# Moving closing copies, output scaling and half sums in a convolution and two-layer network kernel built on fast matrix products

## The chip, the core and the metric

The kernel runs on one core of one Trainium2 chip. The metric is device time in microseconds (us), from the first to the last instruction of the program; lower is better. A core has a matrix engine (TensorE, PE in the profile; its weight loads are listed apart as PEld), a vector engine (VectorE, DVE), a scalar engine (ScalarE, ACT), a general engine (GpSimd, POOL) and a queue engine (SyncE, SP). Each takes its own instructions strictly in the order in which the program lists them, and they wait for one another by semaphores. Matrix products land in PSUM, here eight banks of 512 float32 for each of 128 partitions; everything else lives in SBUF or in DRAM.

## The reference, cut to what matters

```python
# x: (8, 4224, 192), weight: (8 heads, 7 taps)
w = softmax(weight, axis=-1)
y[b, s, 24*h:24*h+24] = sum over k of w[h, k] * x_pad[b, s + k, 24*h:24*h+24]
# x_pad: six zero rows ahead of x, so each row sees itself and the six before it
mu, var = mean and variance of y over its 192 columns
xn = (y - mu) / sqrt(var + 1e-6) * g_ln
out = y + maximum(xn @ w_ch1, 0) @ w_ch2       # (192 x 768), (768 x 192)
```

The factor 1/sqrt(var) passes through the maximum with zero, so the kernel multiplies un-normalised rows and scales the result of the second product. Mean and `g_ln` are folded into the first weight matrix at the start.

## The kernel before

**Groups.** The rows are cut into 18 groups; a full group is 2048 rows, 16 row slots (`J`) for each of 128 partitions. Groups 0 to 2 are small or partial and do ordinary products. Groups 3 to 17 are "mixed": both products of the network are done by a fast scheme with seven products of half-size blocks in place of eight, at the price of sums and differences of blocks ahead of and behind the products. This document is about those 15 groups; the last of them, group 17, does part of its second product in the ordinary way (`down`) and has a short ending of its own.

**A group's first product** is `up_mixed(g)` (lines 585 to 725). It runs in two passes, each with seven calls of `product` (line 521 underneath), each into one of two sets of four PSUM banks, X and Y, in turn:

- pass `one` is the small set: one third of the hidden width (`PAIR` = 2, so f = 2 alone);
- pass `two` is the rest (f = 0 and 1) and takes twice as long.

The hidden layer of a group is one SBUF tile, `room`, seen as `a[:, h, e, f]` with h, e in {0, 1}. Its quarters are called c11 = a[h0, e0], c12 = a[h0, e1], c21 = a[h1, e0] and c22 = a[h1, e1], each with the part of pass one (f = 2) and of pass two (f = 0, 1). A bank set is emptied in one of two ways. `evict` is an ACT copy from PSUM into a quarter. `close` adds a bank set to a quarter that already holds something. A close with a spare part is done as an ACT copy into that part and a POOL-issued DMA that adds the part to the quarter in SBUF (line 583). A close without one is a DVE addition straight from PSUM (line 622). In pass one all three closes have a part; in pass two the first two do, and the last, of c21 from X, is the DVE one. The last group closes everything on DVE.

Before the change the parts of pass one lie in a tile of the pool `tb` (line 647). That pool has one buffer. It also holds, for the group after next, the result of the convolution's second tap (`second_tap`, line 394), which two DMAs add to `y` (line 397). The parts of pass two lie in tiles of the pools `cs` (also the result of the second product) and `tb`.

**The quarters after that.** c12 gets its maximum with zero when it is evicted; c11 and c22 get it by ACT instructions in place (line 629); for c21 `lower_sum` (line 773, DVE) forms max(c21, 0) - c11.

**A group's second product** is `down_fast(g, ...)` (lines 780 to 849), seven calls of its own `product` (line 797), called P1 to P7 below in the order in which they stand. Each is three chunks of columns, and each chunk goes to one bank: P1, P5, P6 and P7 accumulate in banks 0, 2 and 4, P2, P3 and P4 in banks 1, 3 and 5. After each chunk of all but P4 an ACT copy (line 803) takes the bank out. P1 reads c11, P2 the lower sum a[h1, e0], P3 and P5 c22, P4 and P7 c12, P6 c11. Between P4 and P5 nine DVE `half_sum` instructions (line 764) rewrite c22, c11 and c12 in place; the first three write c22, which P5 reads, the next three c11, for P6, and the last three c12, for P7.

**What is woven between.** The engines other than PE also work ahead on the next groups, and the order is written out by hand:

- ACT: two taps of the convolution of group g + 2 (lines 383 and 394), and the scaling of the output of group g - 1, one instruction for each of 16 row slots (`scale`, line 882). When rows 0 to 7 and 8 to 15 are scaled, `add_to_out` (line 889) has POOL issue a DMA that adds them to DRAM, where `y` lies already.
- DVE: taps 2 to 6 of group g + 1 (line 408, 40 instructions for a full group), its `transpose` (line 419), its statistics (`moments`, line 439), sums of its blocks (lines 578 and 579, with 575 and 576 on POOL), and the end of the second product of group g - 1 (`finish_fast`, lines 855 and 857). The transposes of line 857 write the output tile `ot`; its pool has one buffer, so they wait until both `add_to_out` transfers of the group before have read it.

In `down_fast` this weaving was done by `ending(step)` (scaling and adding of g - 1) and `some_taps(n)`.

Of the kernel before, what the change touches and what calls it, by code (L numbers as in the profile page):

```python
# [16 lines left out]
def kernel(  # L17
# [567 lines left out]
    def up_mixed(g, ahead):  # L585


        W = HJ * C
        last = g + 1 == NG
        assert groups[g][2] == 2 * HJ and PAIR * W == 512 and FC == PAIR + 1  # L590
        hidden_tile(g)
        a = ht[g]
        a11, a12, a21, a22 = quarters_of_y(g)
        s1, s2, s3, s4 = ysums[g]
        done = groups[g - 1][2]

        class Pass:
            def __init__(self, f0, f1, chain, other):
                self.n, self.chain, self.other = f1 - f0, chain, other
                self.b11, self.b12, self.b21, self.b22 = quarters_of_w1(f0, f1)  # L600
                self.t = [v[:, :, P * f0 : P * f1] for v in (w1sums[:, k] for k in range(3))]
                (self.c11, self.c12), (self.c21, self.c22) = [
                    [a[:, h, e, f0:f1].rearrange("p f q j t -> p f q (j t)") for e in range(2)]
                    for h in range(2)
                ]

            def product(self, to, left, right, first=True, end=True):
                rows_of_tiles(to, left, right, first, end, True)

            def seen(self, banks):  # L610
                src = banks[:, :, 0 : self.n * W]
                return src.rearrange("p q (f w) -> p f q w", w=W)

            def evict(self, banks, dst, relu=False):
                src = self.seen(banks)
                nc.scalar.activation(dst, src, AF.Relu) if relu else nc.scalar.copy(dst, src)  # L616

            def close(self, c, banks, part=None):


                if part is None or last:
                    nc.vector.tensor_tensor(c, c, self.seen(banks), op=ALU.add)  # L622
                    return
                self.evict(banks, part)
                whole = "p f q w -> p (f q w)"
                add_by_dma(c.rearrange(whole), part.rearrange(whole))

            def relu(self, c):
                nc.scalar.activation(c, c, AF.Relu)  # L629

        def parts(pool, tag):

            room = pool.tile([P, J * D], F32, tag=tag, name=f"parts_{tag}{g}")
            return room.rearrange("p (f q w) -> p f q w", q=NQ, w=W)

        def act_scales(j1, j2):
            if not last:
                scale(g - 1, j1, j2)

        def taps_of_next(*args, **kw):  # L640
            if not last:
                conv(g + 1, *args, **kw)


        X, Y = take_set(), take_set()
        one, two = Pass(PAIR, FC, X, Y), Pass(0, PAIR, Y, X)
        room1 = parts(bpool, "tb")

        p = one
        p.product(X, a11, p.b11, True, False)  # L650
        p.evict(X, p.c11)
        p.product(Y, a12, p.b21)
        p.close(p.c11, Y, room1[:, 0:1])
        p.product(X, s2, p.t[0], False, False)
        p.evict(X, p.c21)
        p.product(Y, s3, p.t[1], True, False)
        p.evict(Y, p.c22)
        p.product(X, s1, p.b12, False, False)
        p.close(p.c22, X, room1[:, 1:2])
        p.product(Y, a22, p.t[2], False)  # L660
        p.close(p.c21, Y, room1[:, 2:3])
        p.product(X, s4, p.b22, False)
        p.evict(X, p.c12, True)

        next(ahead)

        p = two
        room2 = parts(cpool, "cs")
        room3 = parts(bpool, "tb")
        p.product(Y, a11, p.b11, True, False)  # L670
        p.evict(Y, p.c11)
        act_scales(0, 1)
        p.product(X, a12, p.b21)
        p.close(p.c11, X, room2[:, 0:PAIR])
        act_scales(1, 2)
        if last:

            for j1 in (0, HJ):
                part, factor = ots[g - 1][:, j1 : j1 + HJ], rstd[g - 1][:, j1 : j1 + HJ]
                nc.vector.tensor_tensor(  # L680
                    part, part, factor.unsqueeze(2).to_broadcast([P, HJ, D]), op=ALU.mult
                )
                add_to_out(g - 1, j1, j1 + HJ)
        p.product(Y, s2, p.t[0], False, False)
        p.evict(Y, p.c21)
        act_scales(2, 3)
        p.product(X, s3, p.t[1], True, False)
        p.evict(X, p.c22)
        one.relu(one.c11)
        one.relu(one.c22)  # L690
        p.product(Y, s1, p.b12, False, False)
        taps_of_next(2, 5)
        taps_of_next(5, 6, heads=(0, H // 2))
        p.close(p.c22, Y, room3[:, 0:PAIR])
        p.product(X, a22, p.t[2], False)
        taps_of_next(5, 6, heads=(H // 2, H))
        p.relu(p.c11)
        p.close(p.c21, X)
        p.product(Y, s4, p.b22, False)
        p.evict(Y, p.c12, True)  # L700
        lower_sum(g, (PAIR,))
        lower_sum(g, range(PAIR))
        if last:

            rest = a[:, 1, 0, :, :, fast[g] :]
            for f in range(FC):
                nc.scalar.activation(rest[:, f], rest[:, f], AF.Relu)
        taps_of_next(6, K)

        def ending(step):  # L710


            if step == 0:
                two.relu(two.c22)
            if last:
                return
            cuts = [min(j, done) for j in (3, 6, 10, 13, J)]
            if step < len(cuts) - 1:
                scale(g - 1, cuts[step], cuts[step + 1])
            if step == 1:  # L720
                add_to_out(g - 1, 0, 8)
            if step == 3:
                add_to_out(g - 1, 8, done)

        return ending

    po = {}

# [48 lines left out]
        else:  # L777
            half_sum(g, (1, 0), (1, 0), (0, 0), ALU.subtract, fs)

    def down_fast(g, ending):  # L780
        n = fast[g]
        t = width(g)
        w = n * T
# [5 lines left out]
        parts = [free[:, 0:CH], free[:, CH : 2 * CH]]  # L789
        banks = [take_bank() for c in range(CH) for i in range(2)]  # L790

        def product(bank, left, right, to, first):
            for c in range(CH):
                dst = banks[2 * c + bank]
                for f in range(FC):
                    for q in range(NQ):
                        nc.tensor.matmul(  # L797
                            dst[C * q : C * q + C, 0:w], right[:, f, C * c : C * c + C],
                            left[:, f, q], start=(first and f == 0), stop=(f == FC - 1),
                            skip_group_check=True,  # L800
                        )
                if to is not None:
                    nc.scalar.copy(  # L803
                        to[:, c], dst[:, 0:w].rearrange("p (j t) -> p j t", t=t)
                    )

        b = quarters_of_w2()
        c11, c21 = cs[:, 0:CH, 0], cs[:, 0:CH, 1]
        c12, c22 = cs[:, CH:NC, 0], cs[:, CH:NC, 1]
        todo = [(tap, h) for tap in (first_tap, second_tap) for h in range(H)] if g + 2 < NG else []  # L810

        def some_taps(times):
            for tap, h in todo[:times]:
                tap(g + 2, heads=(h, h + 1))
            del todo[:times]

        product(0, a[:, 0, 0], b[0], c11, True)
        ending(0)
        product(1, a[:, 1, 0], w2sums[:, 2], c22, True)
        ending(1)  # L820
        product(1, a[:, 1, 1], w2sums[:, 3], c21, False)
        some_taps(4)
        product(1, a[:, 0, 1], b[2], None, True)
        some_taps(6)
        if g + 1 < NG:
            transpose(g + 1)
            sums = sums_of_y(g + 1, nc.gpsimd)
            next(sums)
            moments(g + 1)
        half_sum(g, (1, 1), (1, 1), (1, 0), ALU.add)  # L830
        half_sum(g, (0, 0), (1, 1), (0, 0), ALU.add)
        half_sum(g, (0, 1), (0, 1), (1, 1), ALU.subtract)
        for c in range(CH):
# [1 line left out]
                c11[:, c], c11[:, c], banks[2 * c + 1][:, 0:w].rearrange("p (j t) -> p j t", t=t),  # L835
                op=ALU.add,
            )
        product(0, a[:, 1, 1], w2sums[:, 1], parts[0], False)
        some_taps(6)
        ending(2)  # L840
        product(0, a[:, 0, 0], w2sums[:, 0], parts[1], False)
        some_taps(len(todo))
        ending(3)
        product(0, a[:, 0, 1], b[3], c12, False)
        if g + 1 < NG:
            next(sums)
        else:
            finish_fast(g, 0, flat, cs, parts)
# [31 lines left out]
    def scale(g, j1, j2):  # L880
        for j in range(j1, j2):
            nc.scalar.mul(ots[g][:, j, :], ots[g][:, j, :], rstd[g][:, j : j + 1])  # L882
# [72 lines left out]
    for g in range(NG):  # L955
# [1 line left out]
        if g + 2 < NG:  # L957
            load_x(g + 2)
        if mixed:
            ending = up_mixed(g, ahead(g))  # L960
        else:
            up(g)
        if not fast[g]:
# [28 lines left out]
            continue  # L992
        if g + 2 < NG:
            store_y(g + 1)
        results = down_fast(g, ending)
        if last:
            finish_fast(g, 1, *results)
            add_and_store(g, slice(0, fast[g]))
# [37 lines left out]
```

## Time and profile before

| | before |
|---|---|
| time, median of 3 runs | 1087.65 us (1085.58 to 1089.54) |
| span of the profiled run | 1085.9 us |
| PE busy | 977.6 us, 90% |
| DVE busy | 893.3 us, 82% |
| ACT busy | 685.6 us, 63% |
| POOL busy | 230.5 us, 21% |
| DMA queue of POOL (q0), share of 16 engines | 46.7% |
| DMA queue of SP (q1), share of 16 engines | 17.1% |
| mean granted TensorE clock | 0.987 |
| first product of group 3 starts at | 123.18 us |
| first product of group 4 | 182.50 us |
| first product of group 16 | 959.12 us |
| first product of group 17 | 1023.04 us |

The profile gives busy time by engine. A PE that counts as busy may still be running its pipeline empty: in a steady group of 65.05 us (376.73 to 441.78) the busy time is 56.66 us. The last rows of the table are start times of the instruction group `ps<-yt,w 32*128 32x256` that opens a mixed group, from the timeline of PE; the difference of two of them is the time of a whole group, whatever happened in it. A line of the timeline gives start, duration, engine, line, operation, output and input, number of instructions, and in brackets the idle time ahead of it with what the profile takes for its releaser. Each float32 matrix product of the program appears as two instructions.

### The profile page before, as it was taken

The page shows a single profiled execution, that of the slowest core. Times are in us where ns is not written, and L with a number is a line of the kernel's source. Part 1 is how long each engine was busy: PE and PEld are TensorE (multiplying, and loading weights), DVE is VectorE, ACT ScalarE, POOL GpSimd, SP SyncE. Part 2 cuts the span into 40 slices and gives each one's busy share as a digit, 9 for nine tenths or more (in the row PEclk, how much of TensorE's full clock was granted, in tenths as well). Part 3 has the DMA queues.
Part 4 walks back from the last instruction along what each step waited for, and adds up shares of the span by engine and source line. Part 5 has one row for each costly group of instructions (what it writes and reads, how often), then busy time and mean ns, then how long its engine had stood idle before and what let it go on. Part 6 is the DMA issues. An engine that isn't in the chain of part 4 may idle for free. (4 is left out here: it accounts for less than half of the span.)

```text
span 1085.9 us, 38303 instructions
## 1 busy us (share of the span) xinstructions
PE 977.6 (90%) x17274; PEld 740.3 (68%) x17274; DVE 893.3 (82%) x1491; ACT 685.6 (63%) x1083; POOL 230.5 (21%) x383
## 2 busy tenths in 40 slices
PE   7999998999888988898899889898898999889998
PEld 5876575857667575675758567585675858567687
DVE  6999986995959879595996959789595986959777
ACT  5646575776757676676776657577475766657361
POOL 1015204121130211311123110412123121130300
PEclk9999999999999999999999999999899999999999
DMA  8352968578585877758668675866768577574331
GB/s 182 105 205 38 241 139 205 108 206 168 169 171 104 222 137 202 147 144 193 135 194 160 189 153 113 218 129 196 147 174 179 119 208 146 128 141 87 58 61 61
DMA packets 26385, 165.14 MB, mean 152 GB/s; under 512 B 3567, under 2 KB 4463, under 8 KB 18542
## 3 DMA queue, kind: packets, MB, share of 16 engines
q0 software_dynamic: 19120, 99.36, 46.7%
q1 hardware_dynamic: 6798, 63.34, 17.1%
q8 instruction: 135, 2.21, 0.8%
q14 instruction: 28, 0.23, 0.1%
q10 hardware_dynamic: 304, 0.00, 0.0%
HBM read 38.95 MB, written 50.33 MB: 82 GB/s over the span
## 5 line engine op out<-in xcount | busy, mean ns | idle before, releaser
L408 DVE SCALAR_TENSOR_TENSOR y<-xg,taps,y 128x384 f32<-128x384 f32 (+3 forms) x734 | 366.9, 580 | 1.0 <-ACT y L383 0.8
L797 PE MATMUL ps<-room,w2sums 128*32 128x256 f32 (+1 forms) x4320 | 241.0, 375 | 17.5 <-DVE room L764 16.5
L521 PE MATMUL ps<-yt,w 32*128 32x256 f32 (+2 forms) x4104 | 240.5, 381 | 0.0
L521 PEld LDWEIGHTS ps<-yt,w 32*128 32x128 f32 x4104 | 208.5, 188 | 25.8 <-issue 7.0
L797 PEld LDWEIGHTS ps<-room,w2sums 128*32 128x32 f32 x4320 | 146.0, 110 | 108.5 <-DVE room L764 34.0
L797 PE MATMUL ps<-room,w 128*32 128x256 f32 (+1 forms) x3240 | 182.6, 378 | 35.7 <-issue 12.6
L797 PEld LDWEIGHTS ps<-room,w 128*32 128x32 f32 x3240 | 112.9, 110 | 100.5 <-issue 17.9
L857 DVE STREAM_TRANSPOSE ot<-cs 128x512 f32<-128x512 f32 (+1 forms) x90 | 55.9, 672 | 152.5 <-DMA out_dram<-ot 104.1
L616 ACT COPY room<-ps 128x1024 f32<-128x1024 f32 (+1 forms) x90 | 129.6, 1440 | 75.9 <-PE ps L521 75.9
L521 PE MATMUL ps<-ysums,w1sums 32*128 32x256 f32 x2160 | 135.0, 395 | 35.7 <-ACT parts_tb L616 35.7
L764 DVE TENSOR_TENSOR room<-room 128x1024 f32<-128x1024 f32 (+1 forms) x135 | 151.9, 1200 | 6.1 <-ACT cs L803 6.1
L521 PEld LDWEIGHTS ps<-ysums,w1sums 32*128 32x128 f32 x2160 | 112.9, 192 | 52.2 <-ACT parts_tb L616 41.4
L803 ACT COPY cs<-ps 128x256 f32<-128x256 f32 (+1 forms) x180 | 63.8, 366 | 99.9 <-PE ps L797 98.0
L616 ACT COPY parts_tb<-ps 128x1024 f32<-128x1024 f32 (+1 forms) x56 | 68.5, 1223 | 57.4 <-DMA y<-tb 44.8
L583 POOL DMA_DIRECT2D room<-parts_tb x56 | 48.3, 862 | 249.9 <-ACT parts_tb L616 177.2
L882 ACT ACTIVATE ot<-ot,r 128x192 f32<-128x192 f32 x232 | 90.9, 449 | 0.0
L629 ACT ACTIVATE room<-room 128x1024 f32<-128x1024 f32 (+1 forms) x60 | 87.5, 1486 | 1.4 <-DMA room<-parts_tb 1.4
L889 POOL DMA_DIRECT2D out_dram<-ot x40 | 35.0, 1098 | 235.5 <-ACT ot L882 205.7
L383 ACT ACTIVATE y<-xg,taps 128x384 f32<-128x384 f32 (+3 forms) x141 | 70.3, 586 | 8.4 <-DMA out_dram<-y 6.9
L521 PE MATMUL ps<-ysums,w 32*128 32x256 f32 x1080 | 65.8, 382 | 6.5 <-ACT parts_tb L616 6.5
L439 DVE BATCH_NORM_STATS2 st<-y 128x6 f32<-128x192 f32 x264 | 69.7, 342 | 0.0
L803 ACT COPY room<-ps 128x256 f32<-128x256 f32 (+1 forms) x90 | 30.2, 364 | 60.6 <-PE ps L797 57.4
(102 smaller groups left out, 897.4 us busy)
## 6 DMA issues: line engine op xcount, KB each, us to landing
xg<-in_x_dram SPq DMA_DIRECT2D x15, 2112.0 KB, 14.8
out_dram<-ot POOLq DMA_DIRECT2D x29, 768.0 KB, 12.3
y<-tb POOLq DMA_DIRECT2D x28, 768.0 KB, 9.1
room<-parts_tb POOLq DMA_DIRECT2D x42, 512.0 KB, 5.5
out_dram<-y SPq DMA_DIRECT2D x13, 1536.0 KB, 6.1
room<-parts_cs POOLq DMA_DIRECT2D x14, 1024.0 KB, 7.5
room<-parts_tb POOLq DMA_DIRECT2D x14, 1024.0 KB, 7.2
xg<-in_x_dram SPq DMA_DIRECT2D x1, 1536.0 KB, 7.9
```

The lines of the kernel that those rows point to most:

```text
L383: nc.scalar.mul(y[g][:, 0:n, cs], xg[g][:, 0:n, cs], taps[:, h, 0:1])
L408: nc.vector.scalar_tensor_tensor(out=y[g][:, 0:n, cs], in0=t[:, k : k + n, cs], scalar=taps[:, h, k : k + 1], in1=y[g][:, 0:n, cs], op0=AL ...
L439: nc.vector.bn_stats(out=sums[g][:, j, :], in_=y[g][:, j, :])
L521: nc.tensor.matmul(banks[:, q, i * w : i * w + w], right[rows, c, P * i : P * i + P], left[rows, :, c, :], start=(first and c == 0 and i = ...
L583: nc.gpsimd.dma_start(out=dst, in_=src, accum_op=ALU.add)
L616: nc.scalar.activation(dst, src, AF.Relu) if relu else nc.scalar.copy(dst, src)
L629: nc.scalar.activation(c, c, AF.Relu)
L764: nc.vector.tensor_tensor(a[:, *dst, f], a[:, *left, f], a[:, *right, f], op=op)
L797: nc.tensor.matmul(dst[C * q : C * q + C, 0:w], right[:, f, C * c : C * c + C], left[:, f, q], start=(first and f == 0), stop=(f == FC - 1 ...
L803: nc.scalar.copy(to[:, c], dst[:, 0:w].rearrange("p (j t) -> p j t", t=t))
L857: nc.vector.transpose(ot[:, 0:n, C * c : C * c + C], flat[:, c].rearrange("p (j t) -> p j t", t=C))
L882: nc.scalar.mul(ots[g][:, j, :], ots[g][:, j, :], rstd[g][:, j : j + 1])
```

## The change

Six edits belong to it. (1) The three closing copies of pass one go to places in `room` that pass two will only write later: the c12 and c22 of pass two. The tile of the pool `tb` for them is gone. (2) In pass two the scaling of the rows of group g - 1 moves by one place each, four rows instead of three are scaled there, and the two `relu` of pass one that stood ahead of the close of c22 move: that of c11 behind this close, that of c22 to the second product. (3) On DVE four of the convolution's instructions move from ahead of the last close to behind it, and the first `lower_sum` moves from behind this close to ahead of it. (4) In `down_fast` one list, `work`, replaces `ending` and `some_taps`. It holds the rest of the `relu`s, the scaling row by row, and the taps, and it is taken from after each chunk, so that the scaling and both `add_to_out` are behind P1 and P2, where they were spread up to behind P6. The `relu` of c22 becomes two halves. (5) Inside a chunk the part f = 2 of pass one is taken first. (6) `moments` and the block sums of the next group move behind the half sums, from ahead of them.

```diff
-        room1 = parts(bpool, "tb")
...
-        p.close(p.c11, Y, room1[:, 0:1])
+        p.close(p.c11, Y, two.c12[:, 0:1])
...
-        p.close(p.c22, X, room1[:, 1:2])
+        p.close(p.c22, X, two.c12[:, 1:2])
...
-        p.close(p.c21, Y, room1[:, 2:3])
+        p.close(p.c21, Y, two.c22[:, 0:1])
...
         p = two
-        room2 = parts(cpool, "cs")
-        room3 = parts(bpool, "tb")
+        rooms = parts(cpool, "cs"), parts(bpool, "tb")
         p.product(Y, a11, p.b11, True, False)
         p.evict(Y, p.c11)
+        p.product(X, a12, p.b21)
+        p.close(p.c11, X, rooms[0][:, 0:PAIR])
         act_scales(0, 1)
-        p.product(X, a12, p.b21)
-        p.close(p.c11, X, room2[:, 0:PAIR])
-        act_scales(1, 2)
...
         p.evict(Y, p.c21)
-        act_scales(2, 3)
+        act_scales(1, 2)
         p.product(X, s3, p.t[1], True, False)
         p.evict(X, p.c22)
-        one.relu(one.c11)
-        one.relu(one.c22)
+        act_scales(2, 3)
         p.product(Y, s1, p.b12, False, False)
         taps_of_next(2, 5)
         taps_of_next(5, 6, heads=(0, H // 2))
-        p.close(p.c22, Y, room3[:, 0:PAIR])
+        p.close(p.c22, Y, rooms[1][:, 0:PAIR])
+        act_scales(3, 4)
         p.product(X, a22, p.t[2], False)
-        taps_of_next(5, 6, heads=(H // 2, H))
+        one.relu(one.c11)
         p.relu(p.c11)
+        lower_sum(g, (PAIR,))
         p.close(p.c21, X)
         p.product(Y, s4, p.b22, False)
         p.evict(Y, p.c12, True)
-        lower_sum(g, (PAIR,))
         lower_sum(g, range(PAIR))
...
+        taps_of_next(5, 6, heads=(H // 2, H))
         taps_of_next(6, K)
-        def ending(step):
...
+        work = [lambda: one.relu(one.c22)]
+
+        def scale_one(j):
+            scale(g - 1, j, j + 1)
+            if j == 7:
                 add_to_out(g - 1, 0, 8)
-            if step == 3:
+            elif j == done - 1:
                 add_to_out(g - 1, 8, done)
...
+        if not last:
+            work += [lambda j=j: scale_one(j) for j in range(4, done)]
+        half = [lambda i=i: two.relu(two.c22[:, i : i + 1]) for i in range(PAIR)]
+        return work[0:11] + half + work[11:]
...
-        def product(bank, left, right, to, first):
+        def product(bank, left, right, to, first, behind=0):
             for c in range(CH):
                 dst = banks[2 * c + bank]
-                for f in range(FC):
+                for f in (PAIR, *range(PAIR)):
...
+                for one in work[:behind]:
+                    one()
+                del work[:behind]
...
-        product(0, a[:, 0, 0], b[0], c11, True)
-        ending(0)
-        product(1, a[:, 1, 0], w2sums[:, 2], c22, True)
-        ending(1)
-        product(1, a[:, 1, 1], w2sums[:, 3], c21, False)
-        some_taps(4)
-        product(1, a[:, 0, 1], b[2], None, True)
-        some_taps(6)
+        product(0, a[:, 0, 0], b[0], c11, True, 3)
+        product(1, a[:, 1, 0], w2sums[:, 2], c22, True, 2)
+        product(1, a[:, 1, 1], w2sums[:, 3], c21, False, 2)
+        product(1, a[:, 0, 1], b[2], None, True, 3)
         if g + 1 < NG:
             transpose(g + 1)
-            sums = sums_of_y(g + 1, nc.gpsimd)
-            next(sums)
-            moments(g + 1)
         half_sum(g, (1, 1), (1, 1), (1, 0), ALU.add)
...
-        product(0, a[:, 1, 1], w2sums[:, 1], parts[0], False)
-        some_taps(6)
-        ending(2)
-        product(0, a[:, 0, 0], w2sums[:, 0], parts[1], False)
-        some_taps(len(todo))
-        ending(3)
+        product(0, a[:, 1, 1], w2sums[:, 1], parts[0], False, 2)
+        product(0, a[:, 0, 0], w2sums[:, 0], parts[1], False, 2)
+        for one in work:
+            one()
         product(0, a[:, 0, 1], b[3], c12, False)
         if g + 1 < NG:
+            moments(g + 1)
+            sums = sums_of_y(g + 1, nc.gpsimd)
+            next(sums)
             next(sums)
```

The list `work` of a full group has 31 entries: the `relu` of c22 of pass one, 12 scalings (rows 4 to 15) with the two halves of the `relu` of c22 of pass two after the tenth of them, and 16 taps. P1 takes three after each chunk, P2 and P3 two, P4 three, P5 and P6 two.

More of the change, by code (lines that the diff above doesn't have):

```diff
@@ L707, in up_mixed @@
                 nc.scalar.activation(rest[:, f], rest[:, f], AF.Relu)
+        taps_of_next(5, 6, heads=(H // 2, H))
         taps_of_next(6, K)
-        def ending(step):
[L713 to L720, printed above, removed]
+        work = [lambda: one.relu(one.c22)]
+        def scale_one(j):
+            scale(g - 1, j, j + 1)
+            if j == 7:
                 add_to_out(g - 1, 0, 8)
-            if step == 3:
+            elif j == done - 1:
                 add_to_out(g - 1, 8, done)
-        return ending
+        if not last:
+            work += [lambda j=j: scale_one(j) for j in range(4, done)]
+        half = [lambda i=i: two.relu(two.c22[:, i : i + 1]) for i in range(PAIR)]
+        return work[0:11] + half + work[11:]
     po = {}
@@ L778, in lower_sum, with down_fast @@
             half_sum(g, (1, 0), (1, 0), (0, 0), ALU.subtract, fs)
-    def down_fast(g, ending):
+    def down_fast(g, work):
         n = fast[g]
@@ L798, in product @@
                             dst[C * q : C * q + C, 0:w], right[:, f, C * c : C * c + C],
-                            left[:, f, q], start=(first and f == 0), stop=(f == FC - 1),
+                            left[:, f, q], start=(first and f == PAIR), stop=(f == PAIR - 1),
                             skip_group_check=True,
@@ L809, in down_fast @@
         c12, c22 = cs[:, CH:NC, 0], cs[:, CH:NC, 1]
[L810 to L815, printed above, removed]
-        product(0, a[:, 0, 0], b[0], c11, True)
-        ending(0)
-        product(1, a[:, 1, 0], w2sums[:, 2], c22, True)
-        ending(1)
-        product(1, a[:, 1, 1], w2sums[:, 3], c21, False)
-        some_taps(4)
-        product(1, a[:, 0, 1], b[2], None, True)
-        some_taps(6)
+        if g + 2 < NG:
+            work += [
+                lambda tap=tap, h=h: tap(g + 2, heads=(h, h + 1))
+                for tap in (first_tap, second_tap) for h in range(H)
+            ]
+        product(0, a[:, 0, 0], b[0], c11, True, 3)
+        product(1, a[:, 1, 0], w2sums[:, 2], c22, True, 2)
+        product(1, a[:, 1, 1], w2sums[:, 3], c21, False, 2)
+        product(1, a[:, 0, 1], b[2], None, True, 3)
         if g + 1 < NG:
             transpose(g + 1)
-            sums = sums_of_y(g + 1, nc.gpsimd)
-            next(sums)
-            moments(g + 1)
         half_sum(g, (1, 1), (1, 1), (1, 0), ALU.add)
@@ L959 @@
         if mixed:
-            ending = up_mixed(g, ahead(g))
+            work = up_mixed(g, ahead(g))
         else:
@@ L994 @@
             store_y(g + 1)
-        results = down_fast(g, ending)
+        results = down_fast(g, work)
         if last:
```

## The prediction

> **What bounds the kernel now.** I read the page first: PE 90% busy, DVE 82%, neither full. Averages over a span don't say which wait ends last, so I went to the timelines of one steady group (376.73 to 441.78, 65.05 us), PE first, to find the places where it stands still:
>
> ```profile
> 376.73 2.87 PE L521 MATMUL ps<-yt,w 32*128 32x256 f32 x48
> 379.53 1.58 PE L521 MATMUL ps<-ysums,w1sums 32*128 32x256 f32 x24
> 383.69 1.58 PE L521 MATMUL ps<-ysums,w1sums 32*128 32x256 f32 x24 [2.58 <-ACT parts_tb L616]
> ...
> 402.16 2.77 PE L521 MATMUL ps<-yt,w1sums 32*128 32x256 f32 x48
> 405.39 2.87 PE L521 MATMUL ps<-ysums,w 32*128 32x256 f32 x48 [0.46 <-ACT parts_tb L616]
> 411.16 4.09 PE L797 MATMUL ps<-room,w 128*32 128x256 f32 x72 [2.89 <-ACT room L616]
> 415.04 7.98 PE L797 MATMUL ps<-room,w2sums 128*32 128x256 f32 x144
> 422.81 4.10 PE L797 MATMUL ps<-room,w 128*32 128x256 f32 x72
> 427.43 0.64 PE L797 MATMUL ps<-room,w2sums 128*32 128x256 f32 x8 [0.53 <-DVE room L764]
> 428.57 0.64 PE L797 MATMUL ps<-room,w2sums 128*32 128x256 f32 x8 [0.50 <-DVE room L764]
> 429.70 7.11 PE L797 MATMUL ps<-room,w2sums 128*32 128x256 f32 x128 [0.49 <-DVE room L764]
> 437.75 4.09 PE L797 MATMUL ps<-room,w 128*32 128x256 f32 x72 [0.94 <-ACT room L803]
> ```
>
> I compare starts with the starts of undisturbed products: 72 instructions in 3.88 us (411.16 to 415.04), 48 in 2.59 (399.57 to 402.16), 24 in 1.39. The losses are then 2.77 at 383.69, 0.64 at 405.39, 3.02 at 411.16, 0.74 + 1.40 around the first chunks of P5, and 1.10 ahead of P7: 9.67 us. What is left, 55.4 us, is a group's PE work.
>
> Then DVE, in the same group:
>
> ```profile
> 374.04 0.96 DVE L855 TENSOR_TENSOR cs<-cs,room 128x768 f32<-128x768 f32 x1
> 387.21 1.90 DVE L857 STREAM_TRANSPOSE ot<-cs 128x512 f32<-128x512 f32 x3 [12.21 <-DMA out_dram<-ot]
> ...
> 391.88 16.98 DVE L408 SCALAR_TENSOR_TENSOR y<-xg,taps,y 128x384 f32<-128x384 f32 x32
> 408.77 2.28 DVE L622 TENSOR_TENSOR room<-room,ps 128x2048 f32<-128x2048 f32 x1
> ```
>
> DVE has one idle stretch in the group, 12.21 us, and from 387.21 on it works without a gap into the next group. So its queue, 52.7 us, runs late: the last close (line 622) begins at 408.77 although the product it needs ended at about 404.8. It ends at 411.05, and P1 starts at 411.16. The profile names ACT as P1's releaser, but that copy ended at 410.21; the close is what came last. The half sums behind P5's stall are late for the same reason. The ring closes through the transfer: half sums late, P6 late, the last scaling behind P6 late, so the transfer of rows 8 to 15 is issued at 374.53 and the transposes wait for it until 387.2. A ring of this kind sets the 65 us; neither PE nor DVE does by its work.
>
> The list of waits says how much of each there is in the run (total us, times, longest):
>
> ```profile
> DVE ot L857 <- DMA out_dram<-ot: 104.1, 9, 12.2
> ...
> DVE ot L857 <- ACT room L616: 46.9, 4, 11.9
> ACT parts_tb L616 <- DMA y<-tb: 44.8, 14, 5.1
> PE ps L521 <- ACT parts_tb L616: 42.2, 28, 4.5
> ```
>
> The third line is the other disease: 14 times (once a mixed group) ACT waits some 3 us for the second tap's transfer to leave the one `tb` buffer, and PE waits behind it (fourth line). The second line is the first again, with its releaser named otherwise (idle 11.95 us of the same kind).
>
> **What the Trainium skill says.** "SBUF — State Buffer", section "SBUF: two separate sides", says VectorE and GpSimd share a port pair as an exclusive lock, which a DVE operation with two SBUF inputs and a GpSimd operation that reads SBUF hold for a whole instruction. That bears on the moved block sums (lines 575, 576). The trace before doesn't show a collision: they ran beside the one-input statistics. "DMA: Bandwidth & Descriptors", section "Anatomy of one DMA — SWDGE (gpsimd) path", puts the semaphore wait of a DMA at the issuing sequencer, so a waiting issue holds up the queue behind it. The trace agrees: POOL sat 205.7 us ahead of its output issues, waiting for ACT. "TensorE: Matmul & The Clock Gate", section "What's actually happening", says activity keeps the clock up and an idle window of about 3.4 us halves it. In windows of 4 us from 560 to 640 and 690 to 900 I find four dips, one right behind a stall of 3.83 us (774 to 778 at 0.50), another behind a shorter one (2.25 us, then 0.57 from 604). A smoother PE should keep these away.
>
> **The change part by part.** I write t = 0 for the end of the product `a22` of pass two (404.75 in the group above).
>
> *Parts of pass one in `room` (edit 1).* Removes the wait for `tb`: 2.77 us of PE. The new homes were last read by P7, P5 and P3, all before the first copy, so ACT doesn't wait. The third part must be read by its DMA before ACT evicts c22 of pass two: issue about 11 us into the group, 5.5 us to land by the page, evict at 23. Cost nothing.
>
> *Pass two on ACT (edit 2).* Evict c22 begins at t = -4.93, as at 399.82, takes 1.76 in a row, the scaling 0.35, and the close of c22 begins as soon as its product is done, t = -2.34, ending -0.48. The last product no longer waits: 0.64 saved. The moved `relu` of c11 follows: scaling to -0.23, then 1.01, so to 0.78.
>
> *The last close (edit 3).* `lower_sum` of pass one now stands ahead of it on DVE and needs that `relu`. This is a new wait, and the close is queued behind it. So DVE runs `lower_sum` from 0.85 to 2.0 (1.16) and the close from 2.0 to 4.3 (2.28), and P1 starts at 4.4, where PE is free at 2.75. New stall: 1.65 instead of 3.02. Bounds: 0, if something earlier frees DVE and `relu`, and 3.
>
> *Work after the chunks (edit 4).* ACT must do, from 4.7 on, P1's three copies (0.27 each in a row), a `relu` (0.93) and eight scalings (0.35): copies can start at 5.95, so it is done with P1's share at about 10.4, P1 itself at 8.3. In P2's share the halves of the c22 `relu` come after the second copy and end near 12.7 and 13.6. P3 starts at 12.2 and needs them after one and two thirds of its first chunk, 12.6 and 13.1: stall about 0.65. Bounds 0 and 2. The six and nine taps behind P3 and P4 (0.51 each) let ACT be level again at about 24, before P6 needs a copy. P7's loss of 1.10 goes.
>
> *The transfers.* Rows 0 to 7 go out at about t = 8.5, 8 to 15 at about 14.5; in the group above it was 15.8 and 34.8 (issues at 420.55 and 439.58). With the page's 12.3 us they land by 27. The second tap's transfers go at 24 to 26 and land by 36 (9.1). Next to them runs the storing of `y` and the loading of x. DMA is full for 14 us in the group above (419.2 to 433.2) and its share over a group is 0.70, thus 0.79 in a group of 57.6: tight, not full.
>
> *Half sums first (edits 5, 6).* From 4.3 DVE does two `lower_sum` (2.3), twelve taps (6.35), the transpose (3.35): 16.3, then waits for P3 to release c22 at 16.7. The nine half sums (10.2) then deliver c22 at 20.1, when P5 can start at 20.6; the losses 0.74 + 1.40 go. POOL's block sums come behind the tap issues, 26 to 29.7, and DVE's statistics end at 32, so nobody waits. If they lock DVE, it is 2 × 1.84 us at most.
>
> *Does DVE keep up?* From 16.7: half sums 10.2, line 834 1.0, statistics 4.15, block sums 1.75, `finish_fast` 5.6, 28 taps 14.8: 54.2. It needs to be there at 57.6 + 0.85. Slack 4 us, with `ot` free at 27 and the taps' `y` complete at 36, where DVE comes at 39.
>
> *Sum.* 55.4 + 1.65 + 0.65 = 57.7 us a group, PE bound. Groups 4 to 15 took (959.12 - 182.50)/12 = 64.72, so 12 × 7.0 = 84. Group 16 took 63.92: 6.2. Group 3 took 59.32, since it has no output of a fast group to wait for: 1.6. The last group closes on DVE in any case: nothing. 92 us in all: 1087.65 - 92 = 996.
>
> **The rivals.**
>
> *PE almost without stalls.* If the two new waits are hidden, a group is 55.4 to 56.2. For it: both estimates rest on tenths of a microsecond in ACT's order. Against: `lower_sum` ahead of the close is in the program. Gain at 55.9: 12 × 8.8 + 8.0 + 3.4 = 117, so 971.
>
> *The transfers or ACT's backlog become the bound.* More work in less time: the DMA queue of POOL is served late, taps start late, DVE's slack of 4 us is used up and 2 us more are lost; 59.7 a group. For it: DMA full for 14 us at a time, landing times up to 14.0 us for the taps. Against: most transfers now start earlier. 12 × 5.0 + 4.2 = 64, so 1023.
>
> *Slower.* The ring stays, because the earlier output transfer queues behind the `y` store and the x load and lands as late as before, and the new wait of the close delays DVE by 1 us a group: 14 × 1 = 14, so 1101. For it: a ring can close again through another transfer. Against: it would need the transfer issued at 14.5 to take over 22 us, where the longest of these in the trace took 15.0.
>
> **How the numbers follow.** 0.60 for 996, 0.14 for 971, 0.18 for 1023, 0.06 for slower, 0.02 for no change. The range is 968 to 1028: it takes in the first three with a few microseconds at each end. Faster 0.92, same 0.02, slower 0.06.
>
> **What would show it.** Right: no wait of line 616 on `y<-tb`; no idle of line 857 on `out_dram<-ot`; a DVE wait ahead of line 773 on ACT line 629 of some 3 to 4 us, and P1 right behind line 622; a short PE wait at P3 on ACT line 629; no waits of P5 on line 764; starts of groups 57 to 58 us apart. Wrong: an idle stretch of over 3 us left on DVE at another place, or a clock well below 0.987.

## The result, and the profile after

The change took the time from 1088.14 us (median of 4 runs, 1085.58 to 1089.54) to 1006.78 us (4 runs, 1005.49 to 1007.84): a ratio of 0.9254, interval 0.9233 to 0.9275. The forecast was 996, its range 968 to 1028. These are the span and the first lines of the page of the kernel after:

```profile
span 1005.1 us, 38307 instructions
PE 958.6 (95%) x17274; PEld 732.5 (73%) x17274; DVE 903.3 (90%) x1491; ACT 683.7 (68%) x1098; POOL 271.4 (27%) x383
```

PE's busy time fell by only 19 us (977.6 before). The span fell by 80.8, so the other 62 us came out of PE's standing still. A steady group (414.45 to 472.19) now takes 57.74 us. Its PE, from the timeline, starting at the last product of pass two:

```profile
439.71 2.77 PE L521 MATMUL ps<-ysums,w 32*128 32x256 f32 x48
444.09 4.09 PE L791 MATMUL ps<-room,w 128*32 128x256 f32 x72 [1.61 <-issue]
447.97 5.21 PE L791 MATMUL ps<-room,w2sums 128*32 128x256 f32 x88
453.49 3.23 PE L791 MATMUL ps<-room,w2sums 128*32 128x256 f32 x56 [0.31 <-ACT room L629]
456.53 4.07 PE L791 MATMUL ps<-room,w 128*32 128x256 f32 x72
460.42 7.95 PE L791 MATMUL ps<-room,w2sums 128*32 128x256 f32 x144
468.19 4.07 PE L791 MATMUL ps<-room,w 128*32 128x256 f32 x72
```

Start to start, as in the prediction, P1 loses 4.38 - 2.75 = 1.63 us, and P2 with P3 8.56 - 7.77 = 0.79. P5 to P7 lose nothing, and no wait for `tb` is left. DVE in the same group, from its timeline:

```profile
416.77 1.90 DVE L846 STREAM_TRANSPOSE ot<-cs 128x512 f32<-128x512 f32 x3
...
440.56 1.22 DVE L767 SCALAR_TENSOR_TENSOR room<-room 128x1024 f32<-128x1024 f32 x1 [4.26 <-ACT room L629]
441.71 2.28 DVE L622 TENSOR_TENSOR room<-room,ps 128x2048 f32<-128x2048 f32 x1
...
456.41 10.31 DVE L758 TENSOR_TENSOR room<-room 128x1024 f32<-128x1024 f32 x9 [0.20 <-PE ps L791]
```

The transposes (now line 846) follow without a gap where they waited 12.21 us. The idle time that is left, but for 0.20 us, is the 4.26 us ahead of the first `lower_sum`: DVE is early and waits for ACT's `relu`. The list of waits of the kernel after has no line for `ot<-out_dram` and none for `y<-tb`. It has three that matter here:

```profile
DVE room L767 <- ACT room L629: 63.5, 14, 5.3
...
ACT room L616 <- DMA room<-room: 7.0, 5, 1.8
...
PE ps L791 <- DVE room L758: 5.3, 2, 2.7
```

The first is the new wait of edit 3. The third, two waits of PE on the half sums of 2.7 us at most, is not in any steady group. They lie in groups 3 and 16. This is the timeline of group 3, three engines:

```profile
163.19 14.00 DVE L758 TENSOR_TENSOR room<-room 128x1024 f32<-128x1024 f32 x9
...
169.69 2.51 POOL L575 TENSOR_TENSOR ysums<-yt 128x768 f32<-128x768 f32 x1
...
172.28 2.69 POOL L576 TENSOR_TENSOR ysums<-ysums,yt 128x768 f32<-128x768 f32 x1
...
177.34 5.67 PE L791 MATMUL ps<-room,w 128*32 128x256 f32 x72 [2.66 <-DVE room L758]
```

The nine half sums took 14.00 us, not 10.31, with POOL's two block sums in the middle of them. PE stood for 2.66 us ahead of P7 and P7 then took 5.60 us to the next group's first product (182.94), where 4.00 is usual (468.19 to 472.19). In group 16 POOL's sums came with the first half sums: those took 13.58 us, PE stood for 2.63 us ahead of P5, and P5 with P6 took 9.48 us for 7.77.

The table splits the spans of the profiled runs by the starts of the first products, for the two kernels and for the experiments below. I compare from the first product of group 3 on: it starts anywhere from 121.66 to 127.12 us in these traces, and of what runs before it the edits touch nothing.

| kernel | group 3 | mean of groups 4 to 15 | group 16 | group 17 to the end | sum |
|---|---|---|---|---|---|
| before | 59.32 | 64.72 | 63.92 | 62.86 | 962.7 |
| after | 61.28 | 58.00 | 62.27 | 63.85 | 883.4 |
| b_parts | 57.47 | 65.05 | 64.45 | 62.85 | 965.4 |
| b_work | 63.38 | 60.56 | 59.92 | 62.86 | 912.9 |
| b_both | 57.30 | 58.00 | 58.03 | 62.94 | 874.3 |
| a_tb | 65.46 | 60.72 | 60.74 | 63.85 | 918.6 |
| a_stats | 62.47 | 62.26 | 63.91 | 63.87 | 937.4 |
| a_dve | 56.84 | 58.02 | 57.66 | 64.19 | 874.9 |
| a_root | 61.38 | 60.18 | 67.26 | 63.91 | 914.7 |
| a_lower | 59.44 | 60.88 | 61.14 | 63.92 | 915.1 |
| lower_dve | 56.12 | 56.77 | 57.43 | 64.53 | 859.3 |
| best1 | 55.43 | 56.70 | 57.30 | 65.34 | 858.4 |
| best3 | 55.48 | 56.37 | 56.21 | 64.68 | 852.8 |

### The profile page after: what moved, and what is told of

Same layout as the page of the kernel before. It is cut to its first block, busy times and chain, and to the rows that moved or that the text cites. A ratio compares the mean times of both kernels' runs of the same rounds, so it can differ in the third digit from the quotient of the medians.

```text
span 1005.1 us, 38307 instructions
## 1 busy us (share of the span) xinstructions
PE 958.6 (95%) x17274; PEld 732.5 (73%) x17274; DVE 903.3 (90%) x1491; ACT 683.7 (68%) x1098; POOL 271.4 (27%) x383
## 4 chain that ended last, share of the span: by engine, by line
PE 58%; ACT 11%; DVE 10%; DMA 9%; POOL 6%; issue 5%; ACTq 0%; DVEq 0%; POOLq 0%
PE ps L521 31%; PE ps L791 21%; DVE room L758 7%; PE ps L738 5%; ACT room L629 5%; DMA room<-room 5%; ACT ot L871 4%; DMA room<-parts_cs 3%; DVE st L439 2%; ACT cs L797 2%; POOL d L457 2%; POOL d L467 1%; DMA xg<-in_x_dram 1%; ACT room L616 1%; POOL r L470 1%
## 5 line engine op out<-in xcount | busy, mean ns | idle before, releaser
L616 ACT COPY room<-ps 128x1024 f32<-128x1024 f32 (+1 forms) x132 | 172.1, 1303 | 90.6 <-PE ps L521 80.6
L521 PEld LDWEIGHTS ps<-yt,w 32*128 32x128 f32 x4104 | 203.6, 185 | 27.7 <-issue 7.0
L758 DVE TENSOR_TENSOR room<-room 128x1024 f32<-128x1024 f32 (+1 forms) x135 | 158.6, 1247 | 10.4 <-PE ps L791 10.4
L521 PE MATMUL ps<-ysums,w1sums 32*128 32x256 f32 x2160 | 123.8, 377 | 0.0
L767 DVE SCALAR_TENSOR_TENSOR room<-room 128x1024 f32<-128x1024 f32 (+1 forms) x45 | 52.8, 1201 | 64.9 <-ACT room L629 63.5
L871 ACT ACTIVATE ot<-ot,r 128x192 f32<-128x192 f32 x232 | 94.6, 455 | 0.0
L383 ACT ACTIVATE y<-xg,taps 128x384 f32<-128x384 f32 (+3 forms) x141 | 74.1, 605 | 7.3 <-DMA out_dram<-y 6.9
L797 ACT COPY room<-ps 128x256 f32<-128x256 f32 (+1 forms) x90 | 33.4, 371 | 66.8 <-PE ps L791 66.8
L521 PE MATMUL ps<-yt,w1sums 32*128 32x256 f32 x1080 | 65.0, 379 | 2.3 <-ACT room L616 2.3
L394 ACT ACTIVATE tb<-xg,taps 128x384 f32<-128x384 f32 x112 | 60.3, 633 | 0.0
```

Source lines behind the costliest of these rows:

```text
L383: nc.scalar.mul(y[g][:, 0:n, cs], xg[g][:, 0:n, cs], taps[:, h, 0:1])
L394: nc.scalar.mul(tb[g][:, 0:n, cs], xg[g][:, 1 : 1 + n, cs], taps[:, h, 1:2])
L521: nc.tensor.matmul(banks[:, q, i * w : i * w + w], right[rows, c, P * i : P * i + P], left[rows, :, c, :], start=(first and c == 0 and i = ...
L758: nc.vector.tensor_tensor(a[:, *dst, f], a[:, *left, f], a[:, *right, f], op=op)
L767: nc.vector.scalar_tensor_tensor(out=a[:, 1, 0, f], in0=a[:, 1, 0, f], scalar=0.0, in1=a[:, 0, 0, f], op0=ALU.max, op1=ALU.subtract,)
L797: nc.scalar.copy(to[:, c], dst[:, 0:w].rearrange("p (j t) -> p j t", t=t))
```

## The experiments

Names with b_ start from the kernel before, the others from the kernel after. Every ratio is against the kernel before, timed beside it on the same chip (medians 1091.63, 1091.24 and 1093.05 us on the three chips used). Two experiments from different chips are compared by ratio and by the table.

### Edit 1 alone: b_parts

```diff
-        room1 = parts(bpool, "tb")
-        p.close(p.c11, Y, room1[:, 0:1])
+        p.close(p.c11, Y, two.c12[:, 0:1])
...
-        p.close(p.c21, Y, room1[:, 2:3])
+        p.close(p.c21, Y, two.c22[:, 0:1])
```

> The kernel before with edit 1 alone (closing copies of pass one in free parts of room). Theory of the ring: the wait of ACT for the second tap's transfer goes (44.8 us in all before), and PE no longer stands still there, but the group is paced by the output transfer that the transposes wait for, so PE only waits longer ahead of P1: 1083 to 1089 us, groups about 64.5 us apart, the idle of DVE ahead of its transposes still some 150 us in all. Rival, each edit gives back the PE wait that it removes: 14 times 2.77 us, so about 1049 us.

Measured: 1091.49 us, ratio 1.0002 (0.9984 to 1.0021). The wait on `tb` that cost PE 2.77 us in each group is gone, and nothing is won. The list of waits of b_parts says where it went:

```profile
DVE ot L856 <- DMA out_dram<-ot: 151.1, 13, 12.5
```

It was 104.1 + 46.9 = 151.0 us before under two names. PE comes earlier to the last close and stands there longer: 5.48 us ahead of P1, where it was 2.89. The ring through the output transfer sets the group.

### Edit 4 alone: b_work

The list `work` replaces `ending` and `some_taps` as in the change, but with the `relu` of c22 whole and first in it (its halves, which edit 4 also brings, are left out), and pass two as before.

```diff
+        work = [lambda: two.relu(two.c22)]
...
+        product(0, a[:, 0, 0], b[0], c11, True, 3)
+        product(1, a[:, 1, 0], w2sums[:, 2], c22, True, 2)
```

> The kernel before with edit 4 alone (one list of work: scaling and output transfers behind P1 and P2, then the taps). The relu of c22 stays whole, four rows less the one that edit 2 moves are scaled in pass two, everything else is as before. Theory of the ring: the output transfer is issued 20 us earlier, DVE's idle of 12 us is gone, the taps' transfer has landed when pass one closes, so the wait for tb goes as well without edit 1; what is left is 0.64 ahead of the last product and about 2.2 us ahead of P5, since the statistics still stand ahead of the half sums: 58.3 us a group, about 1013 us. Rival, each edit gives back the PE wait that it removes: the 1.10 us ahead of P7 alone, about 1072 us.

Measured: 1039.63 us, ratio 0.9538 (0.9506 to 0.957). Most of the gain, but some 27 us short of what I expected, because a new wait took the ring's place. Its list of waits has it; the second line below, the wait for `tb`, was 44.8 us before and is not quite gone:

```profile
ACT room L629 <- DMA room<-parts_tb: 42.0, 14, 4.2
...
ACT parts_tb L616 <- DMA y<-tb: 12.3, 7, 3.3
```

Timeline of b_work, ACT and PE:

```profile
464.62 1.91 ACT L629 ACTIVATE room<-room 128x2048 f32<-128x2048 f32 x1 [3.15 <-DMA room<-parts_tb]
...
470.14 4.09 PE L793 MATMUL ps<-room,w2sums 128*32 128x256 f32 x72 [2.97 <-ACT cs L799]
```

The `relu` of c22 waits for the closing transfer of c22, P1's second copy is queued behind it on ACT, and PE, which needs the banks and c22 for P3, waits 2.97 us. So the change was right to put this `relu` in two halves behind other work.

### Edits 1 and 4 without the rest: b_both

b_work with edit 1, and the `relu` of c22 in halves behind the tenth entry. Edits 2, 3, 5 and 6 are left as before.

> The kernel before with edits 1 and 4 (closing copies of pass one in room; the list of work, with the relu of c22 in two halves behind the tenth scaling), without edits 2, 3, 5 and 6. Theory after the first four runs: the two edits together make nearly the whole gain, because one cuts the ring and the other takes away the wait that this uncovers. Left are 0.64 ahead of the last product, some 0.8 at P3 and some 1.2 to 2.2 at P5 for the half sums behind the statistics: 58.0 to 59.5 us a group, 1008 to 1030 us. Rival: edits 3, 5 and 6 carry much of it, and without them P5 stands as in the run without edit 6 (3.2 us a group): 1045 us or more.

Measured: 1002.93 us, ratio 0.9187 (0.9162 to 0.9213). That is better than I expected and not worse than the whole change (0.9254, interval to 0.9233 at its low end). In the table groups 4 to 15 take 58.00 in both: a steady group takes 57.98 here and 57.73 in the change, but the change loses the difference again in five of the twelve (see a_root). b_both gains 4 us each in groups 3 and 16. Its PE has the small losses of before still in it (timeline of PE):

```profile
442.23 2.87 PE L521 MATMUL ps<-ysums,w 32*128 32x256 f32 x48 [0.51 <-ACT parts_tb L616]
445.03 4.09 PE L793 MATMUL ps<-room,w 128*32 128x256 f32 x72
...
462.27 0.64 PE L793 MATMUL ps<-room,w2sums 128*32 128x256 f32 x8 [0.50 <-DVE room L760]
463.40 7.11 PE L793 MATMUL ps<-room,w2sums 128*32 128x256 f32 x128 [0.50 <-DVE room L760]
```

What it loses there the change loses ahead of P1 (1.63), which here starts at once. So edits 2, 3, 5 and 6 together exchange one set of stalls for another of nearly the same size.

### The change without edit 1: a_tb

```diff
+        room1 = parts(bpool, "tb")
-        p.close(p.c11, Y, two.c12[:, 0:1])
+        p.close(p.c11, Y, room1[:, 0:1])
```

and likewise the other two.

> The changed kernel without edit 1 (closing copies of pass one in a tile of the pool tb again). Theory of the ring: the taps' transfers now land at about the time when the first closing copy wants the tile (417.4 to 418.6 against 417.4 in the trace), so the wait for tb is 0 to 1.2 us a group; on the other side the third closing part no longer lies in c22 and the 0.4 to 0.9 us that the eviction of c22 waits in some groups goes: 1003 to 1018 us. Rival: edit 1 is worth its 2.77 us a group in the new order too: about 1045 us.

Measured: 1045.55 us, ratio 0.9582 (0.9542 to 0.9623). The theory that the shorter ring would let the second tap's transfers land in time fell; the rival was right. Its list of waits has the old line again, `y<-tb`, and its timeline of PE the old stall:

```profile
ACT parts_tb L616 <- DMA y<-tb: 28.8, 10, 4.4
```

```profile
440.48 1.58 PE L521 MATMUL ps<-ysums,w1sums 32*128 32x256 f32 x24 [2.61 <-ACT parts_tb L616]
```

Edit 1 is worth nothing on the kernel before (+2.7 us in the table) and 918.6 - 883.4 = 35 us once the ring is cut. The step from b_work to b_both, 39 us, can't be set beside this: it also brings the halves of the `relu`, and ACT's wait for c22 in b_work (42.0 us) was longer than the one for `tb` (12.3).

### The change without edit 6: a_stats

`moments` and POOL's block sums go back ahead of the half sums.

> The changed kernel without edit 6 (statistics and the block sums of GpSimd ahead of the half sums). Theory: half sums start 4.15 us later, c22 is ready some 3.3 us after P4 ends, so P5 waits for line 758 in each group: 61 us a group, less the collisions of the block sums with the half sums in groups 3 and 16 (about 8 us in all): 1040 to 1050 us. Rival: DVE's slack of 4.3 us ahead of its first lower sum takes it up and nothing is seen: 1005 us.

Measured: 1064.48 us, ratio 0.9756 (0.9722 to 0.979), slower than expected. The stall is P5's, as expected, 3.19 us in the group from 438.49 to 499.62 (61.13 us). The group before it took 62.70, and its P5 and P6, one line in the timeline of PE, show why:

```profile
425.13 9.54 PE L791 MATMUL ps<-room,w2sums 128*32 128x256 f32 x144 [3.19 <-DVE room L758]
```

After the same stall these products ran 9.54 us where the other group's ran 7.98: between 424 and 428 the granted clock was 0.62. In b_both the statistics stand ahead of the half sums too, and P5 waits only twice 0.5 us (1.4 us lost from start to start). The timelines give two reasons: there the half sums begin 1.9 us before P4 ends (459.26 to 461.15), here 0.2 (484.29 to 484.45), as DVE is late behind edit 3's `lower_sum`; and by edit 5 P5 reads f = 2 first, which is the third half sum of c22. So edit 6 mends what edits 3 and 5 bring with them. The two weren't tried apart.

### Block sums on DVE: a_dve

```diff
-            sums = sums_of_y(g + 1, nc.gpsimd)
+            sums = sums_of_y(g + 1, nc.vector)
```

> The changed kernel with the block sums of lines 575 and 576 on DVE in place of GpSimd. Theory: in groups 3 and 16 the two GpSimd sums run beside the half sums and hold these up by 3.3 to 3.7 us (nine half sums 14.0 and 13.6 us there, 10.3 elsewhere); with the sums on DVE behind the statistics the nine take 10.3 us in all groups, groups 3 and 16 take about 57.7, DVE's idle of 4.3 us pays for the 1.9: about 998 us, ratio to the kernel before 0.917. Rival: the two long groups have another cause: 1005 to 1007 us.

Measured: 1004.22 us, ratio 0.9195 (0.9171 to 0.922). All half sums take 10.3 us again. It is faster than the change where POOL met the half sums: group 3 by 4.44 us, group 16 by 4.61. Groups 4 to 15 differ by 0.02 in the mean (the largest single one, group 4, is 0.68 slower), the last group is 0.34 slower. That settles the two slow groups.

### Root of the odd groups behind the closes: a_root

In the change, groups 4, 10, 11, 12 and 14 take 0.3 to 1.0 us more than the 57.73 of the others, 3.3 in all. In the even ones of these ACT waits 1.4 to 1.8 us to evict c22 (`ACT room L616 <- DMA room<-room` above) for the third closing transfer of pass one, whose part now lies in c22 and whose issue is queued on POOL behind `root` of the odd group before. Timelines of POOL (where `root` begins) and ACT in group 10, which starts at 529.92:

```profile
529.69 2.66 POOL L457 TENSOR_TENSOR d<-st 128x32 f32<-128x32 f32 x1 [1.63 <-DVE st L439]
...
551.45 1.86 ACT L616 COPY room<-ps 128x2048 f32<-128x2048 f32 x1 [1.58 <-DMA room<-room]
```

`root` needs the statistics that edit 6 moved behind the half sums, and starts 0.2 us ahead of the group. In b_both, which has edit 1 without edit 6, it starts 7.9 us ahead of group 10 (524.44 and 532.31), in a_stats 9.4 (554.16 and 563.53), and neither list of waits has ACT waiting on `room<-room`. So the wait needs edit 6 as well as edit 1. Here `root` moves behind the three issues.

```diff
+            if g % 2 == 0:
+                root(g - 1)
         yield
...
-            if g % 2:
-                root(g)
```

> The changed kernel with the square root of odd groups (GpSimd, 19 small operations) behind the three closing transfers of the next group's pass one in place of ahead of them. Theory: ahead of them it delays their issue by some 6 us; the third reads its part from c22 of pass two, so ACT waits 1.4 to 1.8 us to evict c22 and PE 0.4 to 0.9 ahead of the last product in five groups; behind them this wait is gone, 3 us in all: 1002 to 1004 us. Rival: it only goes over to the transfer of c11 of pass two, which then comes later: 1006 us or slower.

Measured: 1038.58 us, ratio 0.951 (0.9483 to 0.9537): wrong. The waits of a_root show that ACT's first scaling now waits for `root`, and its timeline of PE that the next eviction and PE are queued behind:

```profile
ACT ot L871 <- POOL r L470: 26.8, 7, 4.0
```

```profile
451.30 4.45 PE L521 MATMUL ps<-yt,w 32*128 32x256 f32 x48 [3.02 <-ACT room L616]
```

I had not counted that ACT's scaling of group g - 1, woven into pass two, needs that very result. The run doesn't test what it was made for.

### First lower sum behind the close again: a_lower

```diff
-        lower_sum(g, (PAIR,))
         p.close(p.c21, X)
...
+        lower_sum(g, (PAIR,))
         lower_sum(g, range(PAIR))
```

> The changed kernel with the first lower sum behind the last close again (the third part of edit 3 undone). Theory: the close begins when its product ends, P1 right behind the last product: 1.61 us a group less there. ACT's share of work after the chunks starts no earlier, so P3 waits longer for the halves of c22, by some 1.0 us. Net 0.5 to 1.0 us a group: 992 to 999 us. Rival: DVE was waiting in any case and the place of the lower sum is of no weight: 1006 us.

Measured: 1043.77 us, ratio 0.9554 (0.9527 to 0.9582), some 32 us slower than the change (ratios, and the table) where I expected it faster. P1 did start at once. But the half sums, in a steady group, now take 14.51 us; the timeline of a_lower:

```profile
474.82 14.51 DVE L758 TENSOR_TENSOR room<-room 128x1024 f32<-128x1024 f32 x9
...
482.99 2.50 POOL L575 TENSOR_TENSOR ysums<-yt 128x768 f32<-128x768 f32 x1
...
485.57 2.67 POOL L576 TENSOR_TENSOR ysums<-ysums,yt 128x768 f32<-128x768 f32 x1
```

P7 then waits 3.07 us (489.47). This is group 3 of the change, here in the steady groups. The timeline of DVE, half sum by half sum, shows two of the nine half sums stretched, to 3.85 and 2.82 us, where all nine take 1.2 in the change. There line 575 also begins within the eighth half sum (464.96; the half sum from 464.36), but it is POOL that pays: 3.45 us for line 575, where the like sum after it takes 1.84. Here it begins 0.26 us into the eighth in place of 0.60, and DVE pays. (The profile gives POOL's times only roughly; both pictures repeat in most of the steady groups.)

### Both: lower_dve

a_lower with the block sums on DVE.

> The changed kernel with the first lower sum behind the last close (as in the run that took 1043.8 us) and the block sums of lines 575 and 576 on DVE. Theory of the shared port: in that run the earlier half sums met the two GpSimd sums in every group (nine half sums 14.5 us, PE 3.1 us idle ahead of P7 and then at half clock); with no GpSimd sums the nine take 10.3, the stall of P7 goes, and what the earlier close saves is seen: 1.6 less at P1, 0.4 to 0.5 more at P3, 56.5 us a group, 980 to 986 us, ratio 0.90. Rival, GpSimd has nothing to do with it and half sums are slow when they run beside P5 and P6: 1035 us or more.

Measured: 987.92 us, ratio 0.9039 (0.9019 to 0.9058). With one word changed in a_lower, 56 us. Half sums of lower_dve, timeline of DVE:

```profile
451.39 10.27 DVE L758 TENSOR_TENSOR room<-room 128x1024 f32<-128x1024 f32 x9
```

So it was POOL beside them that made them 14.5, not their place.

### Smaller stalls: best1 and best3

best1 is lower_dve with the halves behind the fifth entry of `work` (`work[0:5] + half + work[5:]`) and the half sums in the order in which the chunks read them, f = 2 first. best3 also takes the third closing part of pass one out of c22 and puts it into a third of the `tb` tile that pass two uses anyway:

```diff
+        spare = parts(bpool, "tb")
...
-        p.close(p.c21, Y, two.c22[:, 0:1])
+        p.close(p.c21, Y, spare[:, PAIR:FC])
...
-        rooms = parts(cpool, "cs"), parts(bpool, "tb")
+        rooms = parts(cpool, "cs"), spare
```

> As the run before in this list, and the two halves of the c22 relu behind the fifth entry of the work in place of the eleventh, and the half sums in the order f = 2, 0, 1 in which P5 to P7 read them. Theory: P3's wait of about 1.05 us goes, since ACT has both halves done before P2 ends; 55.5 to 55.9 us a group, 970 to 977 us. Rival: the halves now wait for the closing transfer of c22 (ACT stood 3 us a group there in the run with the whole relu first) and hold up ACT's copies of P1: 985 us or more.

> As the last one, and the third closing part of pass one in the tile of the pool tb that pass two uses for its own part (its last third is free) in place of c22 of pass two. Theory: the eviction of c22 no longer waits for the third closing transfer in odd groups (9 us of ACT, about half of it PE), and the tile is free by then, since the taps' transfers land some 3 us ahead of the third close: 3 us less than the last one. Rival: they land later than that, and ACT waits for the tile in all groups: 5 us or more above the last one.

Measured: best1 985.5 us, ratio 0.902 (0.8998 to 0.9042), not to be told from lower_dve: P3's stall went down to 0.2, and the wait of c22's eviction grew to 16.6 us in all (7.0 in the change, 10.9 in lower_dve). best3 took that away: 979.41 us, ratio 0.8962 (0.8944 to 0.898). It beats both kernels. Its even groups keep one new small wait (timeline of PE); the odd ones, all but group 11, take 55.47 us, which is the 55.4 of PE's work:

```profile
437.38 3.66 PE L792 MATMUL ps<-room,w 128*32 128x256 f32 x64 [0.95 <-ACT room L629]
```

## Why the prediction was right, and where it was off

**Right: the ring, and the sum of a steady group.** The prediction had 55.4 + 1.65 + 0.65 = 57.7 us. Measured: 57.74, with 1.63 at P1 and 0.79 at P3, and seven of groups 4 to 15 within 0.01 of it. DVE's slack was put at 4 us and is 4.26. The output transfer no longer holds the transposes, and b_parts and b_work show from two sides that it did hold the group. The losses at P5 and P7 are gone as said.

**The misses, in the prediction's own terms.** It summed 1.6 + 84 + 6.2 = 92 us. The table gives -1.96 for group 3, 12 × 6.72 = 80.6 for groups 4 to 15, 1.65 for group 16 and -1.0 for the last: 79.3; 1.5 came on top because group 3 started sooner.

- *"If they lock DVE, it is 2 × 1.84 us at most"*, and so nobody waits. This is the mis-sized term. In groups 3 and 16 the half sums were 3.7 and 3.3 us longer, PE stood 2.6 us in each, and some 1.6 to 1.7 us more went to the lower clock behind the stall (1.60 at P7 of group 3, 1.71 at P5 and P6 of group 16). a_dve gives the size: 9.05 us for the two. The bound of 3.7 us on DVE held in these groups; in a_lower it did not (4.2). What failed was taking PE's share as nothing: I placed the block sums by a steady group, where they wait behind the taps' issue. In group 3 `work` has 6 scalings in place of 12 (group 2 has ten rows), and in group 16 no taps, so POOL comes earlier, among the half sums. The Trainium skill ("SBUF — State Buffer", section "SBUF: two separate sides") says of this shared port that whichever instruction starts first has it to its end and the other is blocked. That they exclude each other fits; who pays doesn't follow from the starts that the profile gives: in a_lower the eighth half sum started first and was held up.
- *Edit 1: "Cost nothing."* That ACT evicts c22 after the third part was read was given 6.5 us of room: issue at 11, 5.5 to land, eviction at 23. In group 10 the issue began 11.9 us into the group (541.81), landed 9.5 us later, and ACT was ready for the eviction at 20.0. The 23 was read in a group of the kernel before, with the 2.77 us in it that edit 1 itself takes away; and `root`, later by edit 6, was left out (in the odd group from 472.19 the third issue comes at 9.9). Groups 4, 10, 12 and 14 lost 3.0 us. That the eviction waits for that transfer is in the trace, and best3, which removes the cause, is 6 us faster than best1. Of the 0.28 in group 11 I know no cause.
- *The last group: "nothing".* It lost 1.0 us, and in b_both 0.1, so it belongs to edits 2, 3, 5 and 6. Neither edit 6 nor the place of the first `lower_sum` gives it back when undone (63.87 in a_stats, 63.92 in a_lower); the others were not tried.

**Right in sum, wrong in its credit.** The working gave each edit a part of the gain. The runs show that edits 1 and 4 carry all of it: the table's sum falls by 88.4 with them alone, and by 79.3 with all six. The other four together add nothing to a mean group and lose in groups 3, 16 and 17. Undoing edit 6 alone costs 54 us by the table (a_stats), so they lean on one another; edits 2 and 5 were not tried by themselves.

**The rivals.** PE almost without stalls (55.4 to 56.2 a group) was not the change, but it was there to be had: best3 reaches 55.47 in all but one of its odd groups. The transfers as a bound (59.7) didn't come: by the page of the kernel after the output transfer lands in 8.5 us, where it took 12.3. The slower case had nothing for it.

## What to carry to other kernels

Idle time that stands in a ring isn't worth its length: one wait was worth nothing alone and 35 us once the ring beside it was cut, so try each edit both alone and as the only one left out. When work is moved, look at the first and last stages, where the neighbours that kept two engines apart are missing. Two-input sums of VectorE and GpSimd were cheap on two engines here only while something kept them from meeting; moving one instruction of 1.2 us from ahead of a close to behind it turned that into 32 us lost.

## What the runs showed of the hardware that was not expected

- Two GpSimd sums of 1.84 us made nine VectorE sums 3.3 to 4.2 us longer when they met (14.00 in group 3, 13.58 in group 16, 14.51 in a_lower, for 10.3), and themselves became 2.5 to 2.7, but for the first of group 16, which began 0.05 us ahead of the half sums and took 1.84. In the steady groups of the change, where the first of the two met the last two half sums, VectorE lost nothing and GpSimd paid (3.45). What decides between the two I can't say from these runs.
- Stalls of about 2.6 us were followed by a lower granted clock: 0.68 from 178 to 182 us in the kernel after, 0.57 from 928 to 932. By stretches of 1 us it was 0.59, 0.50, 0.50 and 0.70 from 177, and 0.56, 0.50, 0.50 and 0.74 from 928: each time some 3.4 us at half clock, thus 1.7 us of products, which fits the 1.60 and 1.71 lost. The Trainium skill ("TensorE: Matmul & The Clock Gate", section "What's actually happening") puts the idle window at about 3.4 us. Here shorter stalls were followed by it, and not every time: of two stalls of 3.19 us in a_stats, one was followed by a slower product and the other not.
- The small GpSimd instructions of `root` took some 0.45 us each beside VectorE's taps in a_root, and most of them 0.22 to 0.25 beside its transposes in the change; there too they took 0.41 to 0.48 from 422.2 on, when the taps had begun (421.43). `root` as a whole was hardly longer in a_root (10.6 us for 10.0), since in the change its first instruction took 2.7.
